# Cosine-weighted linear attention and a two-layer FFN on one core: another order and other engines for the operations of batches 1 to 8

## The chip, the cores and the metric

The kernel runs on one core of one Trainium2 chip. The core has TensorE (PE, with its weight loads as PEld), VectorE (DVE), ScalarE (ACT), GpSimd (POOL) and SyncE (SP), each working through its own instructions in order. The metric is the device time of one execution in microseconds (us), and the time of a kernel is the median of its runs.

## What is computed

Eight batches of eight heads, 576 tokens of 64 numbers. Linear attention with a cosine weight, then a leaky-ReLU FFN over all 4608 tokens of 512 numbers:

```python
def phi(x, c, s):
    r = np.maximum(x, 0.0)
    return np.concatenate([r * c, r * s], axis=-1)
q_p = phi(q, cos_w, sin_w)
k_p = phi(k, cos_w, sin_w)
kv = np.einsum('bhsf,bhsd->bhfd', k_p, v)
z = np.sum(k_p, axis=2)
num = np.einsum('bhsf,bhfd->bhsd', q_p, kv)
den = np.einsum('bhsf,bhf->bhs', q_p, z)[..., None] + 1e-06
x = num / den                      # to 4608 x 512
...
h = x @ w_in                       # 512 x 2048
g = np.maximum(0.01 * h, h)
return g @ w_out                   # 2048 x 512
```

## The kernel before, in words

The work is cut into nine groups of 512 tokens: groups 0 to 7 hold the first 512 tokens of batches 0 to 7, group 8 the last 64 of all eight. A group's path is as follows. q is loaded to a staging buffer (`qst`), multiplied into `qp` by `q_prep(g,j,...)` (lines 401 and 403, one instruction for the cosine half and one for the sine half) and transposed to `qpT` by a DMA that SP issues (`q_transpose_dma(g,jp)`, L515, two per group). k (`kst`) becomes `kp` by `k_cos` and `k_sin`, nine of each per batch; v is cast to `vm` by `v_pairs`. `kv_sum(b)` (L478) is 72 matmuls of `kp` and `vm` on PE and an eviction on ACT. `num(g,j)` (L565) is 8 matmuls of `qpT` and `kv` (16 in group 8), then three DVE instructions that divide (L576, L580, L581) into `xs`. A DMA transpose (`x_transpose_dma(g)`, L529) makes `xT`. Groups 0, 1 and partly 2 transpose on PE instead.

Both FFN layers of groups 2 to 8, and the second layer of group 1, are seven products where eight blocks would be multiplied, so they need sums of their operands: `x_sum` and `w1_sum` for the first layer, `g_sum` and `weight_sum` for the second. `P(g,u,n)` (L792) is four matmuls of product n of the first layer in unit u of group g; `e(g,u,x)` combines and evicts the three PSUM banks of a unit on DVE and ACT and applies the leaky ReLU (L409, L411, L692, L819). `F(g,i)` (L907) is four matmuls of the second layer; every fourth F of a group is followed by an eviction on DVE or ACT, and the store of a finished quarter of the group's result by a DMA on SP (L966). Four banks, `ps_f`, serve the units of P in turn, three for each; `banks` picks them by a running number. `M` is the first layer of group 1 (512-wide matmuls, L639), `h` and `f2` are the two layers of group 0.

What sets the order is a list written out in the text: `PROGRAM` is a string of such calls, and the last loop of the kernel runs them in the order of the text. A letter D, A or P in a call says that DVE, ACT or POOL does it; a letter in `e` does the same (capitals B, S and U on DVE instead of ACT). Each engine's instructions stand in the order of the list, and so do SP's DMAs (`load`, the transposes and the stores). The tile framework adds the waits that the data and the buffers need.

Staging buffers are four, taken in turn by the loads in the order of the list: a load waits until the last reader of the buffer four loads ago is done. `kp`, `vm` and `xs` exist once, so the casts of batch b wait for `kv_sum(b-1)`. k and v of batch 1, and parts of the weights, are staged in `wext` and `ext`, which later hold sums.

Of the kernel before, what the change touches and what calls it, by code (L numbers as in the profile page):

```python
# [38 lines left out]
f2(2,0,4) load(k,2) k(1,1,2,s,D) k(1,0,1,c,D) f2(3,0,4) f2(0,4,8) v(1,0,1,D) q(1,1,0,8,A) k(1,2,4,c,D,[7.9])
f2(1,4,8) q(1,2,0,8,A) w1_sum(0,1,D) qT(1,0,A,h) f2(2,4,8) qT(1,1,A,h) w2(3,A,2,4) f2(3,4,8) qT(1,2,A,h)  # L40
f2(0,8,12) qT(1,3,A,h) f2(1,8,12) f2(2,8,12) v(1,2,3,D) w2(3,A,0,2) f2(3,8,12) kvps(1,h) kv(1,0,2)
kvo(1,0,2,A) f2(2,12,14) load(k,3) w1_sum(1,1,D) nh(1,0,0,h) dh(1,0,0) nh(1,1,0,h) dh(1,1,0) f2(2,14,16)
q_prep(2,3,0,8,D) f2(3,12,16) f2o(2,A) f2o(3,A) f2(0,12,16) f2(1,12,14) v(1,3,4,P) kvps(1,h) w1_sum(1,2,P)
q_prep(2,1,0,8,P) q_prep(2,2,0,8,A) w1_sum(0,2,D) kv(1,2,4) kvo(1,2,4,A) f2(1,14,15) q_prep(2,0,0,8,A)
xh(1,0,0,h) xh(1,1,0) xho(1,0,D) f2o(0,A) f2(1,15,16) k_sin(2,1,A) load(v,2) f2o(1,A) nh(1,0,1,h) dh(1,0,1)
nh(1,1,1,n) dh(1,1,1) weight_sum(1) k_cos(2,0,D) load(v,3,2,4) k_cos(2,5,P) h(1,[0.1],[0.1],h) xh(1,0,1,o)
k_sin(2,6,D) weight_sum(2) xho(1,1,A,0,1) h(1,[2.3],[0.1],h) xh(1,1,1) k_sin(2,3,A) k_sin(2,5,D) w1_sum(1,4,D)
xho(1,1,A,1,2) q_transpose_dma(2,0) k_sin(2,7,P) k_cos(2,4,A) k_cos(2,8,P) k_cos(2,7,P) k_cos(2,3,A)
k_sin(2,8,P) h(1,[4.5],[0.1],n) q_transpose_dma(2,1) k_cos(2,1,D) load(q,3) k_sin(2,0,A) k_sin(2,2,P)
h(1,[0.1.2.3.4.5],[2.3]) load(v,3,0,2) k_cos(2,6,D) v_pairs(2,0,2,D) store_held() M(1,6) k_cos(2,2,A)  # L50
weight_sum(3) M(1,7) M(1,10) v_pairs(2,2,4,A) k_sin(2,4,D) M(1,11) M(1,8) weight_sum(4) w1_sum(0,3,D) M(1,9)
g_sum(1,1,0,4) kv_sum(2,0,4,n) g_sum(1,1,4,6) k_sin(3,7,D) M(1,12) num(2,0) k_cos(3,2,P) v_pairs(3,2,4,A)
k_cos(3,1,A) M(1,14) w1_sum(0,4,D) k_sin(3,2,D) k_cos(3,0,A) k_sin(3,0,P) k_sin(3,3,A) g_sum(1,2,0,4) M(1,13)
num(2,1) M(1,15) F(1,2) x_transpose(2,0,A) F(1,0) q_prep(3,1,0,8,A) F(1,4) load(q,4) num(2,2) F(1,1)
k_cos(3,3,D) x_transpose(2,1,A) q_prep(3,0,0,8,P) g_sum(1,2,4,6) k_cos(3,6,D) F(1,3) F(1,6) k_sin(3,1,A)
F(1,5) F(1,7) q_prep(3,3,0,8,A) x_transpose(2,2,A) num(2,3) F(1,15) F(1,13) g_sum(1,3,6,8) k_cos(3,7,A)
q_transpose_dma(3,0) k_cos(3,8,P) F(1,12) F(1,10) x_transpose(2,3,A) v_pairs(3,0,2,P) k_sin(3,5,D) F(1,9)
x_sum(2,1,D) F(1,14) q_prep(3,2,0,8,A) k_sin(3,6,A) P(2,0,1) P(2,1,1) x_sum(2,2,D) e(2,0,b) k_cos(3,4,P)
P(2,0,5) load(k,4) k_sin(3,8,D) g_sum(1,4,0,8) k_cos(3,5,P) e(2,0,s) F(1,8) F(1,11) k_sin(3,4,A)
q_transpose_dma(3,1) P(2,0,6) x_sum(2,4,D) load(v,4) x_sum(2,3,D) q_prep(4,0,0,8,P) g_sum(1,3,0,6) e(2,0,u)  # L60
P(2,0,2) kv_sum(3,0,4,n) P(2,0,3) e(2,0,z) P(2,0,7) num(3,0) e(2,0,a) e(2,0,e) e(2,1,b) e(2,0,y) F(1,18)
F(1,17) F(1,16) k_sin(4,0,P) k_sin(4,1,P) F(1,19) q_prep(4,1,0,8,A) P(2,1,6) P(2,1,2) k_cos(4,7,D) e(2,1,u)
k_cos(4,5,D) num(3,1) P(2,1,5) P(2,0,4) F(1,25) e(2,1,s) k_sin(4,2,P) F(1,22) k_cos(4,3,P) k_cos(4,4,P)
# [10 lines left out]
g_sum(2,3,5,8,2) load(q,5) F(2,9) k_cos(5,6,P) g_sum(2,3,0,4,1) P(3,1,5) k_sin(5,2,P) e(3,1,b)
q_transpose_dma(4,1) e(3,0,y) num(4,0) e(3,0,c) F(2,10) P(3,1,6) q_prep(5,2,0,8,P) P(3,1,2) F(2,5)
k_sin(5,3,P) k_sin(5,6,A) e(3,1,u) F(2,6) e(3,1,a) q_prep(5,3,0,8,D) k_cos(5,0,D) k_cos(5,3,A) load(v,5)
k_cos(5,2,D) e(3,1,s) F(2,7) F(2,8) num(4,1) k_sin(5,4,A) k_cos(5,1,A) k_sin(5,0,P) P(3,1,7) F(2,11)
q_transpose_dma(5,1) P(3,2,5) F(2,14) F(2,17) e(3,1,y) g_sum(2,3,4,8,2) P(3,1,3) g_sum(2,4,0,4) num(4,3)
F(2,12) g_sum(2,4,4,8) F(2,18) e(3,2,s) P(3,0,4) F(2,13) e(3,1,z) P(3,1,4) q_prep(5,1,0,8,A) F(2,15) e(3,0,d)
e(3,1,d) e(3,1,c) num(4,2) P(3,2,1) e(3,1,e) q_prep(5,0,0,8,P) e(3,2,b) F(2,16) v_pairs(5,0,2,P)  # L80
x_transpose_dma(4) q_transpose_dma(5,0) F(2,19) P(3,2,3) P(3,2,2) P(3,3,1) k_cos(5,8,A) k_sin(5,1,A) P(3,2,6)
e(3,2,a) P(3,3,5) k_sin(5,7,D) F(2,20) F(2,24) e(3,2,u) P(3,2,7) F(2,26) e(3,2,z) k_cos(5,5,D) e(3,2,y)
F(2,22) g_sum(3,1,0,4,1) k_cos(5,7,A) v_pairs(5,2,4,A) e(3,2,e) e(3,3,b) F(2,21) load(k,6) P(3,2,4) P(3,3,2)
e(3,2,c) k_sin(5,8,D) e(3,2,d) F(2,23) g_sum(3,2,0,4,1) e(3,3,a) P(3,3,6) P(4,0,1) e(3,3,s) e(3,3,u)
g_sum(3,1,4,8,2) g_sum(3,3,0,4,1) kv_sum(5,0,4,n) x_sum(4,1,P) P(3,3,3) x_sum(4,2,D) P(3,3,7) e(3,3,z)
e(3,3,y) num(5,0) k_sin(6,4,P) x_sum(4,3,D) e(3,3,e) load(q,6) F(3,2) g_sum(3,2,4,8,2) P(4,0,5) F(3,0) F(2,25)
P(3,3,4) F(2,27) e(4,0,b) q_prep(6,2,0,8,P) load(v,6) k_sin(6,0,D) e(3,3,c) g_sum(3,3,4,8,2) e(4,0,s)
load(k,7) P(4,0,6) P(4,0,3) P(4,0,2) e(4,0,u) e(3,3,d) e(4,0,z) q_prep(6,0,0,8,P) k_sin(6,3,A) num(5,2)
# [1139 lines left out]
```

## Time and profile before

| | us |
|---|---|
| runs of the kernel before | 275.29, 276.93, 278.28 |
| median | 276.93 |
| the profiled execution's own time | 275.29 |
| its span in the trace | 273.3 |
| busy: PE / DVE / ACT / POOL | 263.6 / 211.5 / 190.2 / 133.2 |

The page of the profile gives the busy time of each engine, the span in 40 slices (a digit is the busy share in tenths), groups of instructions by line with count, busy time and the mean of one in ns, and behind `|` the idle time of the engine just before them with what ended it. The timeline gives start and length of merged instructions, and in brackets the idle time ahead with its releaser. A matmul's recorded length is modelled and reaches past the start of the next one, so distances between starts tell more than busy time.

### The profile page before, as it was taken

What the parts mean: (1) busy time and instruction counts of PE and PEld (TensorE: products, weight loads), DVE (VectorE), ACT (ScalarE), POOL (GpSimd) and SP (SyncE); (2) the same over time, 40 slices, a digit from 0 to 9 for tenths busy, and PEclk for the clock granted to TensorE, in tenths of its full rate; (3) what the DMA queues carried; (4) which work ended last, traced back from release to release, by engine and by line L of the source; (5) the groups of instructions that cost most, each with busy time, mean ns of one, the idle gap of its engine ahead of it and who ended that gap; (6) DMA issues with size and microseconds to landing.
All of it is one profiled execution on the core that took longest, in us unless ns stands there. A gap on an engine that the chain in (4) does not pass through costs nothing.

```text
span 273.3 us, 7194 instructions
## 1 busy us (share of the span) xinstructions
PE 263.6 (96%) x2925; PEld 223.2 (82%) x2925; DVE 211.5 (77%) x427; ACT 190.2 (70%) x337; POOL 133.2 (49%) x103
## 2 busy tenths in 40 slices
PE   8899999999999999899999999999999999999994
PEld 3575555656998998799999999999999899999983
DVE  4851389996999986969979979997989858756762
ACT  7856686997988998596878679565863476573510
POOL 2575025994959993960598429758331004100000
PEclk9999999999999999999999999999999999999998
DMA  7999999996999989989959973981755052201224
GB/s 243 352 395 391 393 398 371 376 231 201 374 225 258 235 246 194 300 172 296 390 181 223 252 176 81 186 197 43 167 109 148 2 78 79 79 0 38 79 64 131
DMA packets 75040, 57.08 MB, mean 209 GB/s; under 512 B 47232, under 2 KB 63616, under 8 KB 74624
## 3 DMA queue, kind: packets, MB, share of 16 engines
q1 hardware_dynamic: 74400, 56.11, 72.7%
q10 hardware_dynamic: 608, 0.52, 0.6%
q8 instruction: 23, 0.38, 0.6%
q14 instruction: 9, 0.07, 0.1%
HBM read 36.70 MB, written 9.44 MB: 169 GB/s over the span
## 4 chain that ended last, share of the span: by engine, by line
PE 66%; DMA 6%; DVE 3%; POOL 1%; issue 0%; DVEq 0%; POOLq 0%
PE ps L907 31%; PE ps_f L792 27%; DMA qpT<-qp 3%; DMA qst<-in_q_dram 2%; PE ps_kv L478 2%; PE ps_num L565 2%; PE ps_h L639 1%; PE ps_f L907 1%; POOL qp L403 1%; DVE ext L692 1%; DVE kp L403 1%; DVE osb L692 0%; PE ps_x L541 0%; DVE s L411 0%; DVE xs L581 0%
## 5 line engine op out<-in xcount | busy, mean ns | idle before, releaser
L907 PE MATMUL ps<-w,g 128*128 128x256 f16 x496 | 68.4, 273 | 1.8 <-DVE ext L692 1.8
L907 PEld LDWEIGHTS <-g 128*128 128x128 f16 x640 | 61.9, 98 | 8.5 <-issue 2.0
L819 ACT ACTIVATE g<-ps_f 128x512 f16<-128x512 f32 x84 | 48.8, 597 | 19.7 <-DVE ps_f L692 11.6
L792 PEld LDWEIGHTS <-w 128*128 128x128 f16 x448 | 48.6, 113 | 1.0 <-issue 0.2
L792 PE MATMUL ps_f<-xT,w 128*128 128x256 f16 x336 | 48.9, 273 | 0.0
L792 PEld LDWEIGHTS <-wext 128*128 128x128 f16 x336 | 36.1, 114 | 0.9
L403 POOL TENSOR_SCALAR qp<-qst,cos_t 128x512 f16<-128x512 f32 (+1 forms) x12 | 24.3, 2028 | 25.4 <-DMA qst<-in_q_dram 14.0
L907 PE MATMUL ps<-T,ext 128*128 128x256 f16 x240 | 33.9, 273 | 0.0
L403 POOL TENSOR_SCALAR kp<-kst,cos_t 128x256 f16<-128x256 f32 (+1 forms) x23 | 27.5, 1200 | 4.6 <-DMA kst<-in_k_dram 3.0
L639 PE MATMUL ps_h<-xT,w 128*128 128x512 f16 (+1 forms) x144 | 29.4, 356 | 0.1
L907 PEld LDWEIGHTS <-ext 128*128 128x128 f16 x256 | 24.8, 98 | 2.5
L792 PE MATMUL ps_f<-X,wext 128*128 128x256 f16 x176 | 26.0, 273 | 0.0
L639 PEld LDWEIGHTS <-w 128*128 128x128 f16 x144 | 15.7, 114 | 10.2
L403 POOL TENSOR_SCALAR qp<-qst,sin_t 128x512 f16<-128x512 f32 (+1 forms) x12 | 24.0, 1999 | 0.0
L692 DVE TENSOR_TENSOR ps_f<-ps_f,u 128x512 f32<-128x512 f32 x28 | 19.4, 693 | 4.0 <-PE ps_f L792 2.3
L403 POOL TENSOR_SCALAR kp<-kst,sin_t 128x256 f16<-128x256 f32 x14 | 19.2, 1379 | 6.6 <-DVE osb L692 6.6
L819 ACT ACTIVATE g<-y 128x512 f16<-128x512 f32 x28 | 17.7, 633 | 5.3 <-DVE y L692 5.2
L692 DVE TENSOR_TENSOR y<-ps_f,s 128x512 f32<-128x512 f32 x28 | 19.1, 682 | 2.2 <-PE ps_f L792 2.0
L409 ACT COPY u<-ps_f 128x512 f32<-128x512 f32 x23 | 13.5, 586 | 9.7 <-PE ps_f L792 9.7
L581 DVE TENSOR_TENSOR xs<-ps_num,rden 128x512 f16<-128x512 f32 x28 | 19.4, 691 | 1.0
L692 DVE TENSOR_TENSOR osb<-ps,ext 128x512 f32<-128x512 f32 x23 | 15.7, 684 | 5.4 <-PE ps L907 5.4
L650 ACT ACTIVATE g<-ps_h 128x1024 f16<-128x1024 f32 x16 | 15.9, 1023 | 5.5 <-PE ps_h L639 5.2
(118 smaller groups left out, 475.2 us busy)
## 6 DMA issues: line engine op xcount, KB each, us to landing
out_dram<-osb SPq DMA_DIRECT2D x32, 256.0 KB, 2.9
qst<-in_q_dram SPq DMA_DIRECT2D x7, 1024.0 KB, 10.0
kst<-in_k_dram SPq DMA_DIRECT2D x6, 1152.0 KB, 8.7
vst<-in_v_dram SPq DMA_DIRECT2D x5, 1152.0 KB, 7.0
w2st<-in_moe_w_out_dram SPq DMA_DIRECT2D x3, 1024.0 KB, 9.8
...
```

What stands on the lines that cost most here:

```text
L403: eng.tensor_scalar(out=o, in0=i, scalar1=0.0, scalar2=col, op0=ALU.max, op1=ALU.mult)
L409: nc.scalar.copy(o, i)
L478: nc.tensor.matmul(ps[:, o, (c - lo) * NE : (c - lo + 1) * NE], lhsT=st["kp", b][sl, c, j, :], rhs=vm[sl, c, j, :], start=(j == 0), stop=( ...
L565: nc.tensor.matmul(ps[lo:hi, h // 4, (h % 4) * NE : (h % 4 + 1) * NE], lhsT=qpT[:, h, lo:hi], rhs=kv[b][:, h, :],)
L581: nc.vector.tensor_tensor(out=xs, in0=ps[:, :, 0 : 4 * NE].rearrange("p a (b e) -> p a b e", e=NE)[:, :, :, 0:D], in1=rden.rearrange("p (a ...
L639: nc.tensor.matmul(ps[:, m % 2, lo:hi], lhsT=w1[m // 4, c][0][:, w1[m // 4, c][1], m % 4 : 512 : 4], rhs=xT[:, lo // P : hi // P, c, :], s ...
L650: nc.scalar.activation(st["g", g][:, m - 1 : m + 1, :], ps, AF.Lrelu)
L692: eng.tensor_tensor(out=o, in0=a, in1=b, op=op)
L792: nc.tensor.matmul(ps[:, mi * HT : (mi + 1) * HT], lhsT=a[:, c, 2 * r0 + mi : 512 : 4], rhs=b[:, c], start=(n in (1, 5) and mi == 0 and c ...
L819: nc.scalar.activation(st["g", g][:, m : m + 2, r * HT : (r + 1) * HT], {"a": A, "c": y22, "e": E, "d": B_}[e].rearrange("p (m t) -> p m t ...
L907: nc.tensor.matmul(ps[:, tt], lhsT=a[:, i, tt * P : (tt + 1) * P], rhs=b[:, i], start=(first and i == 4 * halves[0]), stop=(i == NPR - 1 a ...
```

## The change

The list is another one from the middle of batch 0's first layer on: the calls are the same, but for a few that are cut or joined otherwise, and stand in another order, and many name another engine. The first lines of the text, up to the first numerators of batch 0, stay. Apart from the list, `banks` starts its turn two banks later. Of the list the diff shows one line each:

```diff
-idle(6,o) xh(0,0,0,o) xho(0,0,A,0,1) kvps(0,h) kv(0,2,4) kvo(0,2,4,A) w1(0,0,1,P) w1(0,1,1,P) w1(0,2,2,P)
+idle(6,o) xh(0,0,0,o) xho(0,0,A,0,1) kvps(0,h) kv(0,2,4) kvo(0,2,4,A) w1(0,0,1,P) w1(0,1,1,P) load(w2,0)
...
-        at = 3 * (4 * g + u)
+        at = 3 * (4 * g + u) + 2
```

Over the whole list these counts change: on POOL the instructions that make `qp` go from 26 to 18, the `x_sum` from 11 to 6, the k casts from 34 to 35, `v_pairs` from 3 to 5; on DVE those that make `qp` of groups 1 to 8 from 8 to 22, the k casts of batches 2 to 7 from 40 to 28, the `x_sum` from 17 to 22, `v_pairs` from 1 to 3; on ACT those that make `qp` of groups 1 to 8 from 30 to 24, the k casts of batches 2 to 7 from 34 to 45, `v_pairs` from 8 to 4. PE has the same 2925 matmuls.

First place, SP's queue around the loads of q of batches 4 and 5. Before, `qst_1826` is q of batch 5, `kst_1598` k of batch 5, `qpT_1504` and `qpT_1840` the two transposes of batch 4's q, `xT_1593` group 3's x:

```order
L515 DMA_TRANSPOSE qpT_1504<-qp_1321 128x16x128
L529 DMA_TRANSPOSE xT_1593<-xs_1422 128x16x128
L279 DMA kst_1598<-in_k_dram 128x4x576
L966 DMA out_0_dram<-osb_1621 128x2x256
L966 DMA out_0_dram<-osb_1628 128x2x256
L265 DMA qst_1826<-in_q_dram 128x8x256
L515 DMA_TRANSPOSE qpT_1840<-qp_1762 128x16x128
```

Now `qst_1192` is q of batch 4, `qst_1494` q of batch 5, `vst_1166` v of batch 4, `qpT_1164` and `qpT_1227` the two transposes of batch 3's q, `qpT_1616` the first of batch 4's:

```order
L514 DMA_TRANSPOSE qpT_1164<-qp_1109 128x16x128
L278 DMA vst_1166<-in_v_dram 128x4x576
L264 DMA qst_1192<-in_q_dram 128x8x256
L514 DMA_TRANSPOSE qpT_1227<-qp_1052 128x16x128
L965 DMA out_0_dram<-osb_1233 128x2x256
L965 DMA out_0_dram<-osb_1457 128x2x256
L264 DMA qst_1494<-in_q_dram 128x8x256
L528 DMA_TRANSPOSE xT_1614<-xs_1437 128x16x128
L514 DMA_TRANSPOSE qpT_1616<-qp_1514 128x16x128
```

The load of q of batch 5 moves ahead of both transposes of batch 4's q and of group 3's x. Its buffer is now that of v of batch 3; before it was that of q of batch 4. The load of q of batch 4 (buffer of k of batch 3) now stands between the two transposes of batch 3's q.

Second place, POOL's queue before the key-value sum of batch 2. Before (`qp_790` is q of batch 2, `kp_850` k of batch 2, `kp_1070` k of batch 3):

```order
L692 TENSOR_TENSOR wext_97<-wext_97,w1_2_0_102 128x1024
L403 TENSOR_SCALAR qp_790<-qst_595,cos_t_160 128x8x64
L403 TENSOR_SCALAR qp_790<-qst_595,sin_t_161 128x8x64
L403 TENSOR_SCALAR kp_850<-kst_603,cos_t_160 128x4x64
L403 TENSOR_SCALAR kp_850<-kst_603,sin_t_161 128x4x64
L403 TENSOR_SCALAR kp_850<-kst_603,cos_t_160 128x4x64 x2
L403 TENSOR_SCALAR kp_850<-kst_603,sin_t_161 128x4x64 x2
L403 TENSOR_SCALAR kp_1070<-kst_736,cos_t_160 128x4x64
```

Now (`qp_828` is q of batch 2, `kp_846` k of batch 2, `vm_168<-vst_787` v of batch 2, `kp_1075` k of batch 3):

```order
L402 TENSOR_SCALAR qp_828<-qst_671,cos_t_160 128x8x64
L402 TENSOR_SCALAR qp_828<-qst_671,sin_t_161 128x8x64
L402 TENSOR_SCALAR kp_846<-kst_770,cos_t_160 128x4x64
L410 CAST vm_168<-vst_787 128x18x64
L402 TENSOR_SCALAR kp_846<-kst_770,sin_t_161 128x4x64 x2
L402 TENSOR_SCALAR kp_1075<-kst_862,sin_t_161 128x4x64 x4
```

Three k casts and a weight sum leave POOL here, a v cast comes. The key-value sum itself moves ahead on PE: between `M(1,6)` and it there are now three M's where there were five.

Third place, DVE's queue around its first work on q of batch 5. Before (`qp_1867<-qst_1826`; `ext_96<-ps_7_1805` is an eviction of group 2's second layer):

```order
L581 TENSOR_TENSOR xs_1852<-ps_num_1843,rden_1855 128x512
L403 TENSOR_SCALAR qp_1867<-qst_1826,cos_t_160 128x8x64
L403 TENSOR_SCALAR qp_1867<-qst_1826,sin_t_161 128x8x64
L403 TENSOR_SCALAR kp_1788<-kst_1598,cos_t_160 128x4x64 x2
L692 TENSOR_TENSOR ext_96<-ps_7_1805,ext_96 128x512
L576 TENSOR_SCALAR den_1912<-ps_num_1903 128x8
```

Now (`qp_1811<-qst_1494`; `den_1831` belongs to the first numerator of group 4):

```order
L691 TENSOR_TENSOR g_1244<-g_1244 128x4x256
L402 TENSOR_SCALAR qp_1811<-qst_1494,cos_t_160 128x8x64
L402 TENSOR_SCALAR qp_1811<-qst_1494,sin_t_161 128x8x64
L691 TENSOR_TENSOR ps_f3_1252<-ps_f3_1252,u1_184 128x512
L575 TENSOR_SCALAR den_1831<-ps_num_1821 128x8
```

DVE's first work on q of batch 5 moves from behind the first numerator of group 4 to ahead of it.

More of the change, by code (lines that the diff above doesn't have):

```diff
@@ L39 @@
[L39 to L63, printed above, removed]
@@ L74 @@
[L74 to L88, printed above, removed]
@@ new lines @@
+w1_sum(1,2,D) q_transpose_dma(2,0) k_sin(2,2,A) weight_sum(2) k_sin(2,6,A) h(1,[4.5],[0.1],n) load(v,3,0,2)
+k_cos(2,4,D) v_pairs(2,0,2,D) w1_sum(0,2,D) k_cos(2,0,A) h(1,[0.1.2.3.4.5],[2.3]) M(1,6) k_sin(2,5,A)
+k_cos(2,3,A) k_sin(2,4,A) q_transpose_dma(2,1) k_sin(2,1,P) k_sin(2,3,D) k_cos(2,8,D) k_cos(2,2,D) M(1,12)
+k_cos(2,1,D) M(1,13) k_cos(2,6,D) weight_sum(3) weight_sum(4) M(1,7) kv_sum(2,0,4,n) g_sum(1,1,0,4)
+q_prep(3,2,0,8,A) M(1,8) num(2,0) k_cos(3,4,D) k_cos(3,1,D) M(1,9) M(1,14) F(1,2) q_prep(3,3,0,8,A) num(2,1)
@@ new lines @@
+e(3,0,u) kv_sum(4,0,4,n) g_sum(2,3,0,4,1) P(3,0,3) load(v,5) q_prep(5,2,0,8,D) P(3,0,7) e(3,0,z) k_cos(5,1,P)
+num(4,0) e(3,0,y) x_sum(3,4,D) e(3,0,a) F(2,9) P(3,1,5) e(3,0,e) F(2,4) P(3,1,1) F(2,6) q_prep(5,3,0,8,P)
+e(3,1,b) k_cos(5,8,P) e(3,1,s) F(2,10) g_sum(2,3,5,8,2) P(3,1,6) g_sum(2,2,4,8,2) F(2,8) e(3,1,U) k_sin(5,0,A)
+num(4,1) P(3,0,4) e(3,0,c) P(3,1,2) P(3,1,3) e(3,0,d) P(3,1,7) g_sum(2,3,4,8,2) e(3,1,z) k_cos(5,6,D) e(3,1,a)
+P(3,2,1) P(3,2,5) e(3,1,e) F(2,5) g_sum(2,4,0,4) e(3,1,y) k_cos(5,0,D) e(3,2,b) e(3,2,s) F(2,7) num(4,3)
@@ new lines @@
+q_prep(6,3,0,8,D) k_cos(5,2,D) P(3,3,6) k_sin(5,2,A) F(2,21) g_sum(3,2,0,4,1) P(3,3,2) e(3,2,c) F(2,23)
+e(3,3,u) load(k,6) F(2,25) P(3,3,7) P(3,3,3) e(3,2,d) F(2,26) k_sin(5,5,A) e(3,3,a) e(3,3,y) x_sum(4,1,D)
+e(3,3,z) k_sin(5,8,A) kv_sum(5,0,4,n) P(4,0,1) P(3,3,4) g_sum(3,3,0,4,1) x_sum(4,2,D) P(4,0,5)
+g_sum(3,1,4,8,2) F(2,24) e(3,3,c) num(5,0) load(v,6) x_sum(4,3,P) F(2,27) e(3,3,e) e(4,0,b) P(4,0,6) e(4,0,s)
+P(4,0,2) e(3,3,d) F(3,1) x_sum(4,4,P) num(5,2) F(3,0) q_prep(6,2,0,8,A) P(4,0,3) e(4,0,u) F(3,6) e(4,0,a)
@@ new lines @@
+P(4,3,7) P(5,0,1) e(4,3,z) e(4,2,c) e(4,3,y) k_cos(6,5,D) k_cos(6,4,P) e(4,3,a) P(5,0,5) e(4,3,e)
+g_sum(4,1,4,8,2) e(5,0,s) F(3,23) F(3,26) P(4,3,4) F(3,24) k_sin(6,2,D) x_sum(5,3,D) e(5,0,b) P(5,0,3)
+P(5,0,6) g_sum(4,2,0,4,1) P(5,0,2) q_prep(7,1,0,8,A) e(5,0,u) e(5,0,z) F(4,4) e(4,3,c) F(3,27) P(5,0,7)
+e(4,3,d) k_sin(6,5,P) e(5,0,a) e(5,0,e) kv_sum(6,0,4,n) e(5,0,y) P(5,1,5) P(5,1,1) F(4,6) x_sum(5,4,D)
+e(5,1,b) g_sum(4,3,4,8,2) P(5,0,4) e(5,1,s) q_prep(7,2,0,8,P) g_sum(4,3,0,4,1) num(6,0) P(5,1,6) k_sin(7,3,A)
@@ new lines @@
+P(5,3,4) g_sum(5,1,4,8,2) F(4,23) x_sum(6,4,D) g_sum(5,1,0,4,1) e(5,3,e) e(6,0,b) P(6,0,6) F(4,27) P(6,0,2)
+k_sin(7,5,P) k_sin(7,1,A) e(5,3,c) F(5,0) P(6,0,3) e(5,3,d) q_prep(8,3,0,8,P) e(6,0,u) P(6,0,7)
+kv_sum(7,0,4,n) F(5,2) e(6,0,y) e(6,0,z) F(5,1) F(5,3) num(7,0) e(6,0,a) g_sum(5,2,0,4,1) P(6,1,1) e(6,0,e)
+load_qtail(2) P(6,0,4) F(5,9) e(6,1,B) F(5,8) P(6,1,5) e(6,0,d) P(6,2,1) P(6,1,6) e(6,0,c) e(6,1,s)
+g_sum(5,2,4,8,2) num(7,1) F(5,4) F(5,10) e(6,1,u) P(6,1,7) F(5,11) P(6,1,3) g_sum(5,4,0,4) g_sum(5,3,0,4,1)
```

168 lines of the change are left out of this document (91 added, 77 removed).

## Prediction

> **What bounds the kernel now.** I read the page's head and busy shares first, then the busy time by stretch, then PE's row of the timeline where a stretch has a hole, and from each hole back to what ended it.
>
> ```profile
> span 273.3 us, 7194 instructions
> PE 263.6 (96%) x2925; PEld 223.2 (82%) x2925; DVE 211.5 (77%) x427; ACT 190.2 (70%) x337; POOL 133.2 (49%) x103
> ...
> PE   8899999999999999899999999999999999999994
> ...
> POOL 2575025994959993960598429758331004100000
> ```
>
> ```profile
> 0.00:20.00 20.00, 17.11 (x203) 10.82 (x204) 12.49 (x35) 14.18 (x27) 10.28 (x22) 1.00 0.92 328
> 20.00:60.00 40.00, 39.92 (x318) 22.27 (x317) 27.32 (x48) 31.66 (x49) 21.50 (x15) 1.00 1.06 367
> 60.00:112.00 52.00, 49.41 (x673) 43.67 (x672) 44.84 (x95) 43.74 (x80) 40.64 (x28) 1.00 0.98 249
> 112.00:268.00 156.00, 155.93 (x1731) 145.56 (x1728) 125.89 (x249) 100.67 (x183) 60.79 (x41) 1.00 0.56 142
> 268.00:273.00 5.00, 1.29 (x12) 0.90 (x10) 1.01 (x3) 0.00 (x0) 0.00 (x0) 0.89 0.47 132
> ```
>
> The columns are the stretch, its length, then busy time of PE, PEld, DVE, ACT and POOL with counts, PE's clock, DMA share and GB/s. PE is the bound: from 20 to 60 us it lacks 0.08 us, from 112 to 268 us 0.07 us. The change issues the same 2925 matmuls in other places, so it can only win holes back. Those before 20 us (2.9 us) lie in the part of the list that stays, those behind 268 us are the last results on their way out. That leaves 60 to 112 us, with 2.6 us of idle PE; starts of matmuls tell the holes more exactly, since a matmul's end is modelled past the next one's start.
>
> ```profile
> 60.17 1.46 PE L639 MATMUL ps_h<-xT,w 128*128 128x512 f16 x6
> 61.56 0.23 PE L478 MATMUL ps_kv<-vm,kp 64*128 64x66 f16 x4
> 62.39 1.25 PE L478 MATMUL ps_kv<-vm,kp 64*128 64x66 f16 x68 [0.59 <-POOL kp L403]
> 63.58 0.41 PE L639 MATMUL ps_h<-xT,w 128*128 128x512 f16 x1
> ...
> 86.16 0.60 PE L907 MATMUL ps<-ext,g 128*128 128x256 f16 x4
> 86.96 0.43 PE L565 MATMUL ps_num<-kv,qpT 128*128 128x66 f16 x8 [0.20 <-DMA qpT<-qp]
> 87.23 0.60 PE L792 MATMUL ps_f<-X,wext 128*128 128x256 f16 x4
> ...
> 108.15 0.60 PE L792 MATMUL ps_f<-X1b,wext 128*128 128x256 f16 x4
> 110.55 0.60 PE L907 MATMUL ps<-w,g 128*128 128x256 f16 x4 [1.80 <-DVE ext L692]
> ...
> 261.70 3.22 PE L907 MATMUL ps<-w,g 128*128 128x256 f16 x28
> ```
>
> The last row gives the pitch: 28 matmuls of 256 columns take 3.22 us where four take 0.60, so they start (3.22 - 0.60) / 24 = 0.109 us apart. Six of 512 columns take 61.56 - 60.17 = 1.39 us, 0.23 each; a numerator takes 87.23 - 86.96 = 0.27 us, a key-value sum 63.58 - 62.39 = 1.2 us and its first four. Holes: the key-value sum of batch 2 (four matmuls at 61.56, the fifth at 62.39; four need 0.07) 0.76 us; the numerator num(3,2) 86.96 - 86.16 - 4 x 0.109 = 0.36 us; F(2,14) 110.55 - 108.15 - 0.44 = 1.96 us. Together 3.1 us.
>
> Where the largest comes from:
>
> ```profile
> 96.44 2.31 POOL L403 TENSOR_SCALAR qp<-qst,cos_t 128x512 f16<-128x512 f32 x1
> 98.74 2.47 POOL L403 TENSOR_SCALAR qp<-qst,sin_t 128x512 f16<-128x512 f32 x1
> ...
> 101.24 0.38 SPq L265 DMA_DIRECT2D qst<-in_q_dram  x1
> ...
> 101.24 6.35 DMA qst<-in_q_dram
> ...
> 107.78 0.86 DVE L403 TENSOR_SCALAR qp<-qst,cos_t 128x512 f16<-128x512 f32 x1 [2.48 <-DMA qst<-in_q_dram]
> 108.56 0.47 DVE L403 TENSOR_SCALAR qp<-qst,sin_t 128x512 f16<-128x512 f32 x1
> 108.95 0.95 DVE L403 TENSOR_SCALAR kp<-kst,cos_t 128x256 f16<-128x256 f32 x2
> 109.82 0.67 DVE L692 TENSOR_TENSOR ext<-ps,ext 128x512 f32<-128x512 f32 x1
> ```
>
> The load of q of batch 5 stands in the buffer that q of batch 4 held; its last reader is the POOL pair that ends at 101.21. The load is issued at 101.24 and lands 6.35 us later. DVE has had q_prep(5,3) at its head for 2.48 us; behind it wait two k casts and then the eviction that PE needs. A long GpSimd operation, a late landing and an in-order queue make one hole.
>
> **The change, part by part.** (1) *Key-value sum of batch 2.*
>
> ```profile
> 58.29 4.05 POOL L403 TENSOR_SCALAR kp<-kst,sin_t 128x256 f16<-128x256 f32 x2
> ...
> L403 POOL TENSOR_SCALAR kp<-kst,cos_t 128x256 f16<-128x256 f32 x20 | 24.6, 1236 | 1.6 <-issue 1.6
> L403 POOL TENSOR_SCALAR qp<-qst,cos_t 128x512 f16<-128x512 f32 x11 | 23.0, 2092 | 21.1 <-DMA qst<-in_q_dram 9.6 <-ACT u L409 8.3 <-DMA qpT<-qp 3.2
> ```
>
> POOL's last two of six k casts end at 62.34, which ends the hole. Now POOL has three k casts and one v cast behind the same q pair; four at 1.24 instead of six takes 2.5 us off, against a sum that PE reaches two M's, 8 x 0.23 = 1.8 us, earlier. By this 62.34 - 2.5 - (61.56 - 1.8) = 0.1 us could remain; but a weight sum that stood ahead of the q pair on POOL is now on DVE, which is room on top. The hole goes: -0.76 us.
>
> (2) *q of batch 5.* Its load now takes the buffer of v of batch 3, so no q_prep(4,.) stands ahead of it, and between load and first use lie 132 matmuls at 0.109, two numerators and a key-value sum, 16 us of PE, against 6.35 us: some 9 us of room, of which (3)'s transpose and two stores of results, which now stand ahead of it on SP, take a part. -1.96 us. The first user is again on DVE, so a miss would cost as before.
>
> (3) *num(3,2) and the load of q of batch 4.*
>
> ```profile
> 77.02 0.53 SPq L279 DMA_DIRECT2D kst<-in_k_dram  x1
> 77.66 5.64 SPq L515 DMA_TRANSPOSE qpT<-qp  x1
> ...
> 77.66 9.26 DMA qpT<-qp
> ```
>
> SP gets a new head: the load of q of batch 4 waits for the last k cast of batch 3, and the transpose for num(3,2) stands behind it. A transpose behind one such load took 0.64 + 9.26 = 9.9 us from the load's issue. The casts must be done when kv_sum(3) starts; from there to num(3,2) PE has 1.3 us of that sum, 60 matmuls (6.5 us) and two numerators (0.5 us), 8.3 us. A cast that ends with the sum's start costs 1.6 us, one that ends 1.6 us sooner nothing. The old hole of 0.36 goes in; 0 to 1.6 comes out, and I take 0.7, the middle.
>
> (4) *q of batch 6* waits on SP behind the store of F(2,11)'s result; from there to its use on DVE are 64 matmuls and a numerator, 7.2 us, against 6.35 us for the landing and about 0.6 us for the eviction ahead of it. DVE waits 0 to 1.4 us, taken as 0.3 on PE, nearer to nothing since it only just misses.
>
> (5) *Before 60 us* two w2 loads and q of batch 1 go ahead of k of batch 1. DMA is full there (share 1.06), so bytes only change places. The first half of v of batch 1 comes behind 512 KB more of w2, 1.4 us at that stretch's 367 GB/s, and its cast stands behind a w2 cast on ACT. 0 to 1.4 us, taken as 0.2: PE lacks 0.08 us in the whole stretch, so most such waits are covered by batch 0's products.
>
> (6) *Engines.*
>
> ```profile
> L403 DVE TENSOR_SCALAR qp<-qst,cos_t 128x512 f16<-128x512 f32 x4 | 2.4, 594 | 4.2 <-DMA qst<-in_q_dram 4.2
> ...
> L403 DVE TENSOR_SCALAR kp<-kst,cos_t 128x256 f16<-128x256 f32 x18 | 8.1, 466 | 0.0
> L692 DVE TENSOR_TENSOR X<-xT,X 128x512 f16<-128x512 f16 x6 | 2.7, 445 | 0.0
> L692 POOL TENSOR_TENSOR X<-xT,X 128x512 f16<-128x512 f16 x5 | 5.8, 1169 | 5.7 <-DVE X L692 3.2 <-PE ps_f L792 2.4
> ...
> L403 DVE TENSOR_SCALAR kp<-kst,sin_t x22: 339/349/1245, 54.1 to 172.8; 128x256 f16<-128x256 f32 x22
> ...
> L403 DVE TENSOR_SCALAR qp<-qst,sin_t x9: 345/480/908, 4.9 to 108.6; 128x256 f16<-128x256 f32 x5, 128x512 f16<-128x512 f32 x4
> ```
>
> POOL loses eight q halves (8 x 2.09) and five x sums (5 x 1.17) and gains about 4 us of casts: some 18 us less of 133. DVE gains fourteen q halves (8.3), five x sums (2.2) and sheds twelve k casts (5.6); two copies more and less cancel: about +4.9 us. In 60 to 268 us DVE is busy 170.7 of 208 us, 82%, and goes to 84%. With 37 us of idle time as cover none of it need reach PE; if DVE's waits stay where they are, all 4.9 us do. I take 0.7, near nothing, because PE had holes of 0.07 us in 112 to 268 with DVE at 81%.
>
> Sum on the profiled execution's own 275.29 us (span 273.3, 2.0 us around it): -3.1 for the holes, +0.7 +0.3 +0.2 +0.7 = +1.9, so 274.1. This execution was the fastest of the three; the median is 276.93, 1.64 us above it. What made the others longer is not in this trace; if half of it is the kind of late landing that now has room, half stays: +0.8. **274.9 us**, 0.7% under the median.
>
> [...]
>
> **Rivals.** *A, nothing comes back*: (3), (4) and (6) stay under their covers. For it: POOL has 18 us less and the new order leaves room at the three holes. Against it: (3) has none by my rows. 275.29 - 3.1 + 0.2 + 0.8 = 273.2 us, faster.
>
> *C, DVE becomes the bound*, slower. Place: kv_sum(2) to kv_sum(5), where DVE takes 124 instructions instead of 114. It decides once DVE can no longer run ahead of PE there: then its added 4.9 us land on PE, and if each added half is as long as the longest (0.908 - 0.480 = 0.43, times 14) another 6.0. With (3) to (5) at 1.2 and 0.8 for the spread: 275.29 - 3.1 + 1.2 + 0.8 + 4.9 to 10.9 = 279.1 to 285.1, taken as 281. For it: DVE is at 86% in 60 to 112 us already. Against it: the k casts that leave DVE and ACT.
>
> *D, the late landing only moves*: the transpose behind a load that waits for a buffer misses by more than 1.6, or q of batch 6 does, and a hole like the old one comes back: 274.9 + 2 = 277 us, no change.
>
> **Numbers.** The forecast 0.46, A 0.35, C 0.14, D 0.05. About 1% (2.8 us) is what a measurement of this kernel can tell from no change. Faster by over 1% is A, 0.35; within 1% the forecast and D, 0.51; slower C, 0.14. The range goes from 272.5, A with the spread gone, to 279.5, the near end of C.
>
> **What would show it.** Right: no PE wait for POOL's kp at the second key-value sum, no DVE wait for qst near 100 to 110 us, q of batch 5 issued long before its use, idle PE in 60 to 112 us down from 2.6 to about 1 us, POOL's busy time near 115 and DVE's near 216. For (3), a PE wait for qpT before num(3,2). Wrong: holes between 112 and 268 us that were not there, with DVE named as their end (C), or DVE waiting for qst of batch 6 by more than 1.4 us (D); or a wait in 20 to 60 us for a w2 or v cast, which I priced at 0.2.

## The result and the profile after

| | before | after |
|---|---|---|
| median of 20 runs, us | 275.25 | 276.91 |
| the profiled execution: time, span, us | 275.29, 273.3 | 277.46, 275.6 |
| busy: PE / DVE / ACT / POOL, us | 263.6 / 211.5 / 190.2 / 133.2 | 264.4 / 210.6 / 188.7 / 117.9 |

The ratio after to before is 1.0057, 95% interval 1.003 to 1.0084: 0.6% slower, where 0.7% faster was forecast. It is within 1% and inside the range, but on the other side. The ratios leave out executions more than 1.5% above the fastest of the same kernel (three of the change), the medians hold all.

The page's head and busy shares of the changed kernel:

```profile
span 275.6 us, 7199 instructions
...
PE 264.4 (96%) x2925; PEld 223.3 (81%) x2925; DVE 210.6 (76%) x433; ACT 188.7 (68%) x340; POOL 117.9 (43%) x94
...
PE   8899998999997999999999999999999999999994
...
POOL 2486025957329914973539029928910002000000
```

The busy time by stretch, columns as in the prediction:

```profile
20.00:60.00 40.00, 39.08 (x316) 22.07 (x314) 25.19 (x47) 30.49 (x49) 20.26 (x14) 1.00 1.06 371
60.00:112.00 52.00, 49.34 (x663) 43.04 (x662) 45.49 (x97) 42.83 (x80) 28.66 (x20) 1.00 1.01 244
112.00:268.00 156.00, 155.46 (x1723) 144.79 (x1721) 124.76 (x251) 101.60 (x187) 58.10 (x40) 1.00 0.55 141
```

POOL lost its 15 us, and PE still lacks 2.7 us in 60 to 112 us (2.6 before), 0.9 us in 20 to 60 us (0.08 before) and 0.5 us behind 112 us (0.07 before). From starts of matmuls, counting what is above 0.12 us from 20 us on, the holes are 3.7 us before and 5.6 us after; with some 0.5 us more ahead of 20 us (the 200th matmul starts at 20.08 instead of 19.57) that accounts for the 2.3 us by which the spans differ. The two large holes of before are gone, and three others stand in their place. In PE's row of the timeline:

```profile
45.38 0.46 PE L1006 MATMUL ps_kv<-vm,kp 64*128 64x66 f16 x18 [0.71 <-POOL vm L410]
...
71.10 0.43 PE L564 MATMUL ps_num<-kv,qpT 128*128 128x66 f16 x8 [0.66 <-DVE xs L580]
...
87.24 0.60 PE L906 MATMUL ps<-w,g 128*128 128x256 f16 x4
89.83 0.43 PE L564 MATMUL ps_num<-kv,qpT 128*128 128x66 f16 x8 [1.99 <-DMA qpT<-qp]
```

They are 0.88 us in the key-value sum of batch 1, 0.83 us before num(2,3), and the largest, 89.83 - 87.24 - 4 x 0.109 = 2.16 us, before num(3,2). SP's row and the chain of waits of the changed kernel say where that one comes from (the length of an SPq row is the time for which the issue keeps SP, that of a DMA row runs to the landing):

```profile
74.71 0.58 SPq L278 DMA_DIRECT2D vst<-in_v_dram  x1
77.23 0.39 SPq L264 DMA_DIRECT2D qst<-in_q_dram  x1
77.73 7.96 SPq L514 DMA_TRANSPOSE qpT<-qp  x1
```

```profile
77.73 12.05 DMA qpT<-qp
89.78 0.05 issue
89.83 0.43 PE ps_num L564 x8
```

The transpose stands behind the load of q of batch 4, as step (3) said, but takes 12.05 us and not 9.26. The place is right, the size isn't. Two loads are under way ahead of it, not one: v of batch 4, issued at 74.71, landed at 81.75, and q of batch 4 at 85.88.

### The profile page after: what moved, and what is told of

Its sections match the earlier page's. It is cut to its first block, busy times and chain, and to the rows that moved or that the text cites. A ratio compares the mean times of both kernels' runs of the same rounds, so it can differ in the third digit from the quotient of the medians.

```text
span 275.6 us, 7199 instructions
## 1 busy us (share of the span) xinstructions
PE 264.4 (96%) x2925; PEld 223.3 (81%) x2925; DVE 210.6 (76%) x433; ACT 188.7 (68%) x340; POOL 117.9 (43%) x94
## 4 chain that ended last, share of the span: by engine, by line
PE 68%; DMA 18%; DVE 8%; POOL 2%; issue 1%; SPq 1%; ACT 0%; POOLq 0%; DVEq 0%
PE ps L906 31%; PE ps_f L791 27%; DMA ext<-in_v_dram 5%; DMA w2st<-in_moe_w_out_dram 5%; DMA qpT<-qp 4%; PE ps_h L638 4%; DMA kst<-in_k_dram 3%; PE ps_num L564 2%; PE ps_kv L477 2%; DVE qp L402 2%; DVE ext L691 2%; PE ps_f L906 1%; DVE xs L580 1%; POOL kp L402 1%; POOL vm L410 1%
## 5 line engine op out<-in xcount | busy, mean ns | idle before, releaser
L906 PE MATMUL ps<-w,g 128*128 128x256 f16 x496 | 67.7, 273 | 0.1
L818 ACT ACTIVATE g<-ps_f 128x512 f16<-128x512 f32 x84 | 48.2, 598 | 19.5 <-PE ps_f L791 10.8
L402 POOL TENSOR_SCALAR kp<-kst,cos_t 128x256 f16<-128x256 f32 (+1 forms) x19 | 23.0, 1217 | 19.4 <-PE ps_kv L477 9.9
L402 POOL TENSOR_SCALAR kp<-kst,sin_t 128x256 f16<-128x256 f32 x19 | 24.9, 1316 | 7.9 <-PE ps_kv L477 4.0
L402 POOL TENSOR_SCALAR qp<-qst,cos_t 128x512 f16<-128x512 f32 (+1 forms) x7 | 14.1, 2013 | 17.8 <-DMA qpT<-qp 12.0
L691 POOL TENSOR_TENSOR xT<-xT 128x512 f16<-128x512 f16 x3 | 3.8, 1267 | 34.3 <-DVE X L691 28.9
L906 PE MATMUL ps<-ext,g 128*128 128x256 f16 x128 | 18.2, 272 | 0.0
```

The lines of the kernel that those rows point to most:

```text
L402: eng.tensor_scalar(out=o, in0=i, scalar1=0.0, scalar2=col, op0=ALU.max, op1=ALU.mult)
L691: eng.tensor_tensor(out=o, in0=a, in1=b, op=op)
L818: nc.scalar.activation(st["g", g][:, m : m + 2, r * HT : (r + 1) * HT], {"a": A, "c": y22, "e": E, "d": B_}[e].rearrange("p (m t) -> p m t ...
L906: nc.tensor.matmul(ps[:, tt], lhsT=a[:, i, tt * P : (tt + 1) * P], rhs=b[:, i], start=(first and i == 4 * halves[0]), stop=(i == NPR - 1 a ...
```

## The experiments

Twelve kernels, each timed beside the kernel before, whose median was 275.25 to 276.01 us from call to call; so ratios are compared. "Dipped" is the number of executions whose mean granted clock was under 0.9955, of all executions; the kernel before dipped in 17 of its 110 in the calls of E1 to E12.

| kernel | us | ratio to before, interval | dipped |
|---|---|---|---|
| the change | 276.91 | 1.0057, 1.003 to 1.0084 | 4 of 20 |
| E1 transpose ahead of both loads | 275.93 | 1.0015, 0.9985 to 1.0045 | 2 of 12 |
| E2 weight sums later | 276.98 | 1.0057, 1.0021 to 1.0093 | 3 of 12 |
| E3 half of v of batch 3 on DVE | 276.68 | 1.001, 0.9972 to 1.0047 | 3 of 12 |
| E4 former banks | 276.09 | 1.0027, 0.9998 to 1.0055 | 0 of 12 |
| E5 transpose between the loads | 277.34 | 1.0068, 1.0024 to 1.0111 | 6 of 12 |
| E6 = E5 and k of batch 6 | 278.02 | 1.0073, 1.0038 to 1.0107 | 8 of 12 |
| E7 = E6 and both contentions | 278.66 | 1.0104, 1.0047 to 1.0162 | 3 of 6 |
| E8 kernel before, q product later | 275.57 | 0.9995, 0.9962 to 1.0027 | 1 of 12 |
| E9 = E6 and q of batch 4 | 274.97 | 0.9974, 0.9951 to 0.9997 | 1 of 12 |
| E10 = E9 and both contentions | 275.25 | 0.9989, 0.9956 to 1.0021 | 0 of 12 |
| E11 = E6 with the hole filled | 276.14 | 1.002, 0.9989 to 1.0051 | 0 of 12 |
| E12 = E9 without k of batch 6 | 275.95 | 1.0002, 0.9973 to 1.0032 | 1 of 12 |

**E1, the transpose ahead of both loads** (steps of `PROGRAM` that don't matter are left out in these diffs):

```diff
+q_transpose_dma(3,1)
 load(v,4)
...
 load(q,4)
...
-q_transpose_dma(3,1)
```

> The changed kernel (276.9 us) with one step moved on SyncE alone: the second transpose of q of batch 3 stands ahead of the load of v of batch 4 instead of behind that load and the load of q of batch 4. Theory 1 (the changed kernel loses its time at three waits that it made: num(3,2) 2.16 us, kv_sum(1) 0.88, num(2,3) 0.83): the transpose lands before its numerator is reached, the hole of 2.16 us at num(3,2) is gone, and the time is 274.7 us, about 0.5 below the kernel before (ratio 0.998). Rival 1 (the DVE or another engine is the bound there, the hole only names the last of several waits): what the transpose gives comes back within the next microseconds, 276.4 to 276.9 us (ratio 1.004 to 1.006). Rival 2 (the loads pushed behind the transpose are late in turn): a wait for v or q of batch 4 appears behind 90 us and the time is 276 or more.

By the ratios it gained 1.0057 - 1.0015 = 0.4%, 1.2 us, half of what theory 1 wanted, and the intervals overlap. The transpose landed in time, and the hole came back 1.6 us later, at num(3,3). The timeline of POOL, DVE, ACT and PE of E1 there:

```profile
87.23 2.12 POOL L691 TENSOR_TENSOR w<-w,w 128x1024 f16<-128x1024 f16 x1
...
87.25 2.25 DVE L402 TENSOR_SCALAR kp<-kst,cos_t 128x256 f16<-128x256 f32 x1
...
89.57 0.72 ACT L400 ACTIVATE qp<-qst,cos_t 128x512 f16<-128x512 f32 x1 [2.29 <-DMA qst<-in_q_dram]
...
91.19 0.43 PE L564 MATMUL ps_num<-kv,qpT 128*128 128x66 f16 x8 [1.71 <-DVE xs L580]
92.03 0.60 PE L791 MATMUL ps_f<-X,wext 128*128 128x256 f16 x4 [0.42 <-ACT ps_f L408]
```

Both rivals were half right. v of batch 4 now lands late, so POOL starts its weight sum 3 us later, 0.02 us ahead of DVE's cast of k, and the cast takes 2.25 us where the same one takes 0.35 in the changed kernel. And ACT waits 2.29 us for q of batch 4 in front of an eviction. E1's chain of waits goes through that load, which took longer than the 8.65 us (85.88 - 77.23) of the changed kernel:

```profile
80.14 9.41 DMA qst<-in_q_dram
```

**E2, the sums of weights later:**

```diff
-weight_sum(1) w1_sum(0,1,D)
 v(1,2,3,D)
+weight_sum(1) w1_sum(0,1,D)
```

> The changed kernel with two DVE operations moved: the sums of the second layer's and the first layer's weights that now run while GpSimd casts v of batch 1 stand behind DVE's own cast of v. Theory 1 with contention (a DVE sum of two SBUF operands and a GpSimd instruction hinder each other): GpSimd's cast of v of batch 1 takes 1.0 us instead of 2.38, the hole of 0.88 us in kv_sum(1) is gone or under 0.2, and the time is 276.0 to 276.2 us (ratio to the kernel before about 1.003). Rival (the cast is long since its data is still on its way, or for GpSimd's own reasons): the cast stays at 2 us or more and the time at 276.9. A second rival: the moved sums are late for their users, and a wait takes the place of the hole.

The cause of the hole is confirmed, and the gain that theory 1 expected did not show (the ratio is the change's; a gain of 0.3% would lie within the intervals). POOL's two casts of v in the changed kernel, with the DVE sum that ran beside them, and in E2:

```profile
42.94 3.00 POOL L410 CAST vm<-ext 128x576 f16<-128x576 f32 x2 [4.09 <-DMA ext<-in_v_dram]
42.98 1.22 DVE L691 TENSOR_TENSOR T<-w 128x2048 f16<-128x2048 f16 x1
```

```profile
43.14 0.67 POOL L410 CAST vm<-ext 128x576 f16<-128x576 f32 x1 [4.09 <-DMA ext<-in_v_dram]
44.66 0.67 POOL L410 CAST vm<-ext 128x576 f16<-128x576 f32 x1 [0.85 <-DMA ext<-in_v_dram]
...
52.10 1.02 PE L638 MATMUL ps_h<-xT,w 128*128 128x512 f16 x4 [1.04 <-DVE xT L410]
```

A cast takes 0.67 us in E2, and the first of the two took 2.38 us beside DVE's sums in the changed kernel. The hole is gone, but the 1.9 us of sums on DVE now delay an eviction, and PE waits 1.04 us for it at 52 us (second rival).

**E3, half of v of batch 3 on DVE:**

```diff
-v_pairs(3,2,4,P)
...
 num(2,3)
+v_pairs(3,2,4,D)
```

> The changed kernel with the cast of the second half of v of batch 3 done by DVE behind num(2,3) instead of by GpSimd ahead of it. Theory 1 with contention: the second sum of g for M(1,15) on DVE takes 0.4 us instead of 1.32, num(2,2)'s divide is early by as much, the hole of 0.83 us before num(2,3) is gone, and the time is 276.1 us (ratio about 1.003). Rival (DVE is at its limit in this stretch, and the instruction added to it, about 0.6 us, moves the hole): a hole of 0.4 to 0.8 us behind num(2,3) and 276.5 to 277 us.

The time is undecided: the interval reaches from below the kernel before to the change's. The wait itself was as the theory has it. In the changed kernel POOL's cast and DVE's sum of g lie on each other:

```profile
68.58 1.14 POOL L410 CAST vm<-vst 128x1152 f16<-128x1152 f32 x1 [0.98 <-DMA vst<-in_v_dram]
...
68.69 1.32 DVE L691 TENSOR_TENSOR ext<-ext,g 128x512 f16<-128x512 f16 x1
```

In E3 that sum took 0.42 us, and the hole at num(2,3) fell from 0.83 to 0.33 us. But the hole before P(4,1,2) grew from 0.56 to 1.56 us. ACT and PE of E3:

```profile
132.64 0.51 ACT L400 ACTIVATE kp<-kst,cos_t 128x256 f16<-128x256 f32 x1 [2.24 <-DMA kst<-in_k_dram]
...
134.28 0.60 PE L791 MATMUL ps_f<-xT,w 128*128 128x256 f16 x4 [1.39 <-ACT ps_f L408]
```

ACT waits for k of batch 6 in front of an eviction; what PE gains ahead of it, it waits there.

**E4, the former banks:**

```diff
-        at = 3 * (4 * g + u) + 2
+        at = 3 * (4 * g + u)
```

> The changed kernel with the former running number of the PSUM banks of the first layer's products (without the added 2), and nothing else. Theory 1 (the order and the engines make the whole difference): no change beyond 0.3 us, 276.6 to 277.2 us, and the same three holes. Rival (the other banks for the first product of each unit make waits for evictions): 275.3 to 276.3 us, with fewer holes behind 112 us.

With this number the second layer of the last group takes banks that still hold products, so part of its result isn't the reference's; the work is the same. The holes are those of the change (1.76 us at num(3,2), 0.67 at P(4,1,2)); so the places are theory 1's and the time is the rival's. The intervals overlap that of the change, so the banks' share is not told apart; by the medians it would be some 0.8 us.

**E5 and E6, the transpose between the loads, and k of batch 6.** E5:

```diff
 load(v,4)
...
+q_transpose_dma(3,1)
 load(q,4)
...
-q_transpose_dma(3,1)
```

> The changed kernel with the second transpose of q of batch 3 between the load of v of batch 4 and the load of q of batch 4, so that v of batch 4 is not late as it was with the transpose ahead of both. Theory 2 (the waits are real, but the gain of one is partly given back by the next late landing: k of batch 6, for which ScalarE waits in front of an eviction that PE needs at P(4,1,2)): the transpose lands near 84 to 86 us, the hole of 2.16 us at num(3,2) is gone, no long DVE cast of k appears near 87 us, and the hole before P(4,1,2) grows from 0.56 to 1.0 to 1.6 us; 275.2 to 275.8 us (ratio to the kernel before 0.999 to 1.001). Theory 1 (holes add up): 274.7 us. Rival (an engine is the bound): 276.4 us or more.

E6 adds:

```diff
 q_transpose_dma(5,0)
+load(k,6)
...
-load(k,6)
...
-k_cos(6,3,A)
...
 e(4,1,s)
+k_cos(6,3,A)
```

> The same, and k of batch 6 made harmless: its load stands ahead of two stores of results on SyncE, and the ScalarE cast that waits for it stands behind the evictions of unit 1 of group 4. Theory 2: both holes are gone, 276.9 - 2.16 - 0.56 = 274.2 us (ratio 0.996), and the difference to the run before is what the landing gave back. Rival (what is given back has another cause, an engine): the hole at P(4,1,2) goes but another of the same size comes behind it, and the time equals that of the run before.

Neither was faster than the change; their intervals overlap with its, and theory 2 had wanted 1 to 2.7 us less. Only E5's rival had the time, and for another reason. Num(3,2) no longer waits, and P(2,2,6) waits 2.48 us instead. E6's chain of waits, PE's row there, and its busy time by stretch:

```profile
80.70 0.89 SPq L514
...
81.71 6.90 DMA qst<-in_q_dram
88.61 0.03 issue
88.63 1.33 ACT qp L400 x2
89.97 0.49 ACT g L818
90.46 0.02 issue
90.48 0.58 ACT ps_f L408
```

```profile
91.10 0.60 PE L791 MATMUL ps_f<-X,wext 128*128 128x256 f16 x4 [2.32 <-ACT ps_f L408]
```

```profile
89.00:91.00 2.00, 0.00 (x0) 0.00 (x0) 1.87 (x4) 1.97 (x5) 2.00 (x2) 1.00 1.02 343
91.00:92.00 1.00, 0.90 (x8) 0.81 (x8) 0.00 (x0) 1.00 (x4) 1.00 (x2) 0.85 2.03 192
92.00:95.00 3.00, 3.00 (x16) 2.14 (x15) 0.70 (x1) 2.08 (x5) 3.00 (x2) 0.50 0.75 155
95.00:96.00 1.00, 1.00 (x10) 0.90 (x9) 0.81 (x2) 0.56 (x1) 0.12 (x1) 0.94 1.14 216
```

Two things are to be seen. The transpose held SP for 5.99 us, and the load of q of batch 4 went out at 81.71, 4.5 us later than in the changed kernel; ACT has the product of that q ahead of two evictions. That gives theory 3, as E9's expectation has it below: whichever of the two comes second on SP is late, and either one stops PE. And in 89 to 91 us PE is idle, and from 92 to 95 us its granted clock is 0.50: 16 matmuls instead of some 27. By these rows the clock is down for about 3.4 us (0.15 / 0.5 + 3 + 0.06 / 0.5), which costs 1.7.

**E7, both contentions as well** (E6 with the edits of E2 and E3, and `q_prep(2,0,0,8,D)` behind `xho(1,0,D)`):

> The same, and the two places at which DVE and GpSimd hinder each other: the two sums of weights behind DVE's cast of v of batch 1 (with the DVE product for q of batch 2 put behind the eviction of group 1's first transposes, since the moved sums made that one late), and the second half of v of batch 3 cast by DVE. Theory 2 with contention: the holes at kv_sum(1), 51.5 us and num(2,3) go as well, 0.88 + 0.36 + 0.83 us, all in all 276.9 - 2.16 - 0.56 - 2.07 = 272.1 us (ratio 0.989), the fastest of all. Rival (DVE is at its limit by then): within 0.7 us of the run before.

The expected 272.1 was far off: the hole at P(2,2,6) is 3.2 us there. PE came to it only 0.2 us sooner than in E6 (its numerator ahead starts at 88.13 instead of 88.35), and ACT's product of the same load began 0.5 us later (89.15 instead of 88.63).

**E8, the kernel before with one operation moved:**

```diff
-q_prep(5,3,0,8,D)
 k_cos(5,0,D)
...
 num(4,1)
+q_prep(5,3,0,8,D)
```

> The kernel before, with one operation moved: DVE's two products for q of batch 5 stand behind num(4,1) instead of ahead of two casts of k and the eviction that PE waits for at F(2,14). If that hole's cause is the in-order queue behind the late landing: the hole of 1.96 us goes, and the time is 275.3 - 1.96 = 273.3 us (ratio 0.993), which is all that the changed order wins there. Rival (the gain is given back by a later landing or by the engines): a new hole behind 110 us and a ratio of 0.997 to 1.000.

The rival's time held: the interval leaves out the 0.993 that was expected, though not a gain of up to 1 us. The 1.96 us hole at F(2,14) is gone, and PE of E8 has small holes around it that were not there:

```profile
103.04 0.60 PE L792 MATMUL ps_f<-xT,w 128*128 128x256 f16 x4 [0.51 <-ACT u L409]
...
104.42 0.60 PE L792 MATMUL ps_f<-X1b,wext 128*128 128x256 f16 x4 [0.29 <-ACT g L819]
...
111.51 0.43 PE L565 MATMUL ps_num<-kv,qpT 128*128 128x66 f16 x8 [0.30 <-DMA qpT<-qp]
```

By starts they are 0.7, 0.5 and 0.5 us, and 0.9 us lie at 132 to 135 us (0.2 before). The first two come ahead of the moved operation and can't be its consequence; why they came in this execution stays open.

**E9 to E11, the wait itself and the clock.** E9 is E6 with:

```diff
-q_prep(4,1,0,8,A)
 num(3,2)
...
 q_prep(4,0,0,8,D)
+q_prep(4,1,0,8,A)
```

> The run with the transpose between and k of batch 6 made harmless, and one ScalarE operation moved: the product for q of batch 4, which waits for its load at the head of ScalarE's queue, stands behind the evictions of unit 2 of group 3 instead of ahead of them. Theory 3 (of the transpose and the load of q of batch 4 whichever comes second on SyncE is late, because a transpose holds SyncE until the loads ahead of it have landed; the hole is 2.2 us at num(3,2) or 2.5 us at P(2,2,6), and only taking the waiting operation out of ScalarE's way ends it): no hole above 1 us near 88 us, no execution with a dip of the granted clock there, and 273.9 us (276.4 us, the median of the undipped executions of the run without this, minus 2.5; ratio 0.993). Rival (an engine is the bound): a hole of like size behind it, 276 us or more.

E10 adds the edits of E2 and E3, with `q_prep(2,0,0,8,D)` behind `dh(1,0,1)`:

> The same, and the two places at which DVE and GpSimd hinder each other: the sums of weights behind DVE's cast of v of batch 1, the DVE product for q of batch 2 between the two divisions of group 1's second half, and the second half of v of batch 3 cast by DVE. Theory 3 with contention: the holes at kv_sum(1) (0.9 to 1.5 us) and num(2,3) (0.1 to 0.8 us) go as well, 272 to 272.8 us (ratio 0.986 to 0.989), faster than both kernels. Rival: within 0.7 us of the run before.

E11 is E6 with:

```diff
-        for mi in range(2):
+        for mi in (0, 1) * (5 if (g, u, n) == (2, 2, 5) else 1):
```

> The run with the transpose between and k of batch 6 made harmless, with the hole of 2.5 us at P(2,2,6) filled: one product of that unit, P(2,2,5), is multiplied five times instead of once (1.75 us of matmuls more, the same result), so that PE is idle for 0.6 us instead of 2.3 and waits for the same eviction. Theory on the clock (an idle time of PE above some 2 us at this place makes the granted clock fall to a half for 3.4 us afterwards, in two of three executions, which costs 1.7 us each): no execution below a mean clock of 0.9955 for that reason, and 276.4 us instead of 278.0 (ratio 1.002), though PE does more work. Rival (the clock falls for a reason of its own, as by the load on PE): as many dipped executions as before, 278 us or more.

Theory 3 holds for the place: the long hole is gone. The gain is smaller than expected (0.9974 and not 0.993). E9 has the lowest ratio of all and is clearly faster than the change and E6. Against the kernel before it is 0.26%, with an interval that ends just under 1, which among twelve kernels can come by chance. Its SP, ACT and PE rows at the place:

```profile
83.92 0.51 SPq L264 DMA_DIRECT2D qst<-in_q_dram  x1
...
88.72 0.57 ACT L408 COPY ps_f<-ps_f 128x512 f32<-128x512 f32 x1
...
91.23 0.73 ACT L400 ACTIVATE qp<-qst,cos_t 128x512 f16<-128x512 f32 x1
...
93.64 0.60 PE L791 MATMUL ps_f<-xT,w 128*128 128x256 f16 x4 [0.56 <-ACT g L818]
```

The load goes out later still, and the two evictions no longer stand behind it; in their place a hole of 0.72 us comes at 93.64, where PE waits for an ACT operation behind the moved product. E9 missed its expected 273.9 by 1.1 us. E10 won nothing on E9: the hole in the key-value sum of batch 1 was absent in E9's profile too, and in E10 PE waits 0.88 us for DVE's division at 53 us. This suggests that from 44 to 53 us PE waits for DVE's whole chain, and that the cast of 2.38 us was only where it showed; no run tests that. E11 came out at 276.14 against 276.4 expected: a PE that multiplies 1.75 us more is 1.9 us faster by the medians (of two calls; the ratios differ by 0.5%, and their intervals just overlap). None of its 12 executions dipped, against 8 of 12, and the four of E6 that did not dip have a median of 276.4, so it is the clock that it won back (the kernel before dipped about as often in both calls, 5 and 3 of 29). E11's busy time by stretch:

```profile
86.00:92.00 6.00, 5.23 (x60) 5.04 (x58) 4.24 (x11) 3.47 (x7) 6.00 (x6) 1.00 1.04 351
92.00:96.00 4.00, 4.00 (x39) 3.88 (x38) 3.07 (x7) 3.16 (x8) 3.44 (x2) 1.00 0.75 142
```

**E12, E9 without its part on k of batch 6** (the second diff of E6 undone):

> The fastest run so far (transpose between, q of batch 4 behind the evictions, k of batch 6 made harmless) with the last of its three parts undone: the load of k of batch 6 and the ScalarE cast that waits for it stand where the changed kernel has them. If part of what the first two parts win is given back there: no hole above 1 us near 88 us, a hole before P(4,1,2) of 1.0 to 2.0 us with ScalarE's eviction behind the wait for k of batch 6 as its end, and 275.8 to 276.5 us (ratio to the kernel before 1.000 to 1.003). Rival (k of batch 6 gives nothing back, the part is idle ballast): 274.9 us, ratio 0.9974.

It measured 275.95, in the expected band, with a hole of 0.86 us before P(4,1,2) that E9 doesn't have (1.0 to 2.0 was expected). The intervals of E9 and E12 overlap, so the size (0.3%) is less sure than the sign. E12's ACT and PE:

```profile
131.53 0.51 ACT L400 ACTIVATE kp<-kst,cos_t 128x256 f16<-128x256 f32 x1 [1.47 <-DMA kst<-in_k_dram]
...
133.18 0.60 PE L791 MATMUL ps_f<-xT,w 128*128 128x256 f16 x4 [0.70 <-ACT ps_f L408]
```

## Why the prediction was wrong, point by point

- **Steps (1) and (2)** were right in their waits and not in their price: there is no PE wait for POOL's kp at the second key-value sum, and q of batch 5 goes out at 86.9 us instead of 101.2. But in E8 taking (2)'s hole away alone is worth nothing that can be measured, 0.1 us by its ratio and at most 1.0 by its interval, so -1.96 was a hole's length and not a gain.
- **Step (3)** is the one that failed, and decides the sign. I priced "a transpose behind one such load" at 9.9 us from the load's issue and took 0.7, at most 1.6. It took 89.78 - 77.23 = 12.55 us, and PE lost 2.16. The load did not go out too late. It went out when ACT's cast of v of batch 3 ended, 2.1 us ahead of kv_sum(3), which starts at 79.33, and by my range nothing would have been lost then. (The last cast of k of batch 3 ran to 78.96, so the load did not wait for it, and did not stand in k's buffer, as I had it there and in the description of the change.) What was too small is the 9.9: with the load of v of batch 4 still under way the load of q took 8.65 us, where the load in my rows took 6.41. It took 9.41 in E1, issued 0.7 us behind that load of v, and 6.90 in E6, where v landed just as it was issued. And the step hides a second wait: with the transpose put first, ACT's product of q of batch 4 stops PE for 2.5 us (E6). I had put what stands behind the transpose on SP into the sum, and not what stands behind the load's first reader on ACT. With both taken away (E12, E9) the ratio falls from 1.0057 to 1.0002 and 0.9974, and E9's interval doesn't meet that of the change. That these two waits make the kernel slower is shown. They are not the whole miss: E12 without them is as fast as the kernel before and not 0.7% faster, and in its profile smaller holes, some 3.0 us from 20 us on against 3.7 before, stand where (1) and (2) took theirs away.
- **Step (4)** was right in its range: no hole at the first use of q of batch 6, for which 0.3 was taken. Its own sum, 6.35 + 0.6 against 7.2 us, already left room.
- **Step (5)** was taken as 0.2 and measured 0.88 at kv_sum(1), for another reason than the forecast one: v of batch 1 landed at 42.8 us and the cast itself took 2.38 us instead of 0.67. In E2, without this hole, the ratio is the same, though its interval doesn't rule out so small a gain.
- **Step (6)**: POOL's 117.9 came about as forecast (115); DVE's +4.9 did not come (210.6 after 211.5). The added halves came, and other groups got shorter. The sums of g that changed most, before and after:

```profile
L692 DVE TENSOR_TENSOR ext<-g 128x512 f16<-128x512 f16 x16 | 9.5, 601 | 2.0 <-ACT g L819 1.2 <-ACT g L650 0.8
```

```profile
L691 DVE TENSOR_TENSOR ext<-g 128x512 f16<-128x512 f16 x16 | 6.7, 417 | 0.0
```

  Another group of these sums, `ext<-ext,g` of 128x512, got longer, from 6.6 to 8.0 us, so it is not shown that DVE met fewer GpSimd instructions. The 0.83 us at num(2,3) is a price of (6) that I had not: one sum of g at 1.32 us beside a GpSimd cast, where the same sum took 0.42 in E3 with no GpSimd instruction beside it. Two more pairs were seen: in E1 DVE's cast of k took 2.25 us beside POOL's weight sum of 2.12 us and ended 0.15 us behind it, where the same cast took 0.35 beside POOL's casts of k in the changed kernel; and there POOL's cast of v took 2.38 beside DVE's sums instead of 0.67 in E2.
- **The spread, +0.8**, had no ground: over 20 runs the median of before is 275.25, the time of its profiled execution but for 0.04. Against that median the forecast of 274.9 is 0.1% faster; most of the 0.7% was the 276.93 of three runs.
- **Rivals.** A was refuted by (3). C was not borne out: DVE's busy time didn't rise. D named the mechanism, and I gave it 0.05. With (3) at 2.16 the mechanism was D's. That its 277 is almost the time measured is luck: it is the forecast plus 2, and holds the 3.1 us of holes as a gain and the +0.8.

What E8's small holes come from, what share the banks have, and whether moving ACT's product alone would do without moving the transpose, stays open.
